# Moving the first batch's transform on chip, with a first MLP block of plain products

## The chip, the cores and the metric

One core of one Trainium2 chip runs the kernel alone. The metric is the device time of one launch in microseconds (us), as the median of several executions. The experiments ran on several chips of the same kind; each was timed beside executions of the kernel before on its own chip, and ratios are against those.

## The reference

Eight batches of 3008 tokens by 256 channels are filtered in the frequency domain, and the result goes through an MLP with a hard-swish. All is float32.

```python
def _attn_ref(x, filt_r, filt_i):                 # x (8, 3008, 256)
    X = np.fft.rfft(x, axis=1)
    Y = X * (filt_r + 1j * filt_i)[None, :, :]
    return np.fft.irfft(Y, n=x.shape[1], axis=1).astype(np.float32)

def _moe_ref(x, w_in, w_out):                     # x (24064, 256), w_in (256, 2048), w_out (2048, 256)
    h = x @ w_in
    g = h * np.clip(h + 3.0, 0.0, 6.0) / 6.0
    return (g @ w_out).astype(np.float32)
```

## The kernel before

The Fourier transform over 3008 = 47 x 64 tokens is done in stages on TensorE. `a_unit` transforms over 47; its output goes to DRAM (`z_tmp`) and comes back in another layout. `b_unit` transforms over 64, `f_unit` multiplies by the filter on VectorE, `y_unit` adds the products up, and `bi_unit` is the first inverse stage. Its output goes through DRAM again (`g_tmp`, loaded by `t4_load`), and `n_unit` is the last inverse stage, which feeds the MLP.

The MLP works on 47 blocks of 512 tokens, in eight steps each (one per 256 hidden columns). A block uses Strassen's scheme: seven 2x2-block products in place of eight, for which VectorE and GpSimd form sums of inputs and weights. The weights come as 64-bit floats and are converted by VectorE with integer operations (`w_conv`).

The first batch is transformed before the MLP starts, in a prelude, and the other batches' stages are spread over the MLP's steps by a plan, `at(step, function, ...)`. The other batches' stages are spread over the MLP's steps by a plan: `at(step, function, ...)`.

```python
        for c in range(NB):                          # prelude, cut
            a_unit(0, c)
            z_store(0, c, (nc.sync, nc.scalar))
            ...
        convert(6)
        for c in range(TB):
            t2_load(0, c)
            ...
        for i in range(NU + 1):
            if i < NU:
                b_unit(0, i)
                f_unit(0, i)                         # three products on VectorE
                y_unit(0, i)                         # two sums on VectorE
                if i % 3 == 2 and i < NU - 1:
                    convert(1)
            ...                                      # bi_unit, g_store, table_load
        ...                                          # t4_load, n_unit; then the MLP
            if n == 1:                               # places of batch 2's stages, in MLP steps
                a_at = list(range(NB))
                b_at = [10 + 7 * i // 4 for i in range(NU)]
            ...
            for c in range(NT):
                s = ... if c >= TB else a_at[-1] + 1
                at(s, t2_load, n, c)                 # nc.sync.dma_start(t, z_d[...])
                s = ... if c >= FB else a_at[-1] + 1
                at(s, table_load, n, c)              # five loads on nc.sync
        ...
            if dn and pd == 0 and kd:                # in the step after a block's last
                out_5(kd - 1)                        # ends with store(): 14 DMAs a block on nc.sync
```

Of the kernel before, what the change touches and what calls it, by code (L numbers as in the profile page):

```python
# [22 lines left out]
N = 3008  # L23
NA = 47
# [30 lines left out]
def _make_tables():  # L55
# [3 lines left out]
    wai = np.zeros((P, HC, TOK))  # L59
    for h in range(2):  # L60
        for k in range(KH):
            th = 2 * np.pi * ((a * k) % NA) / NA
            for g in range(2):
                wa[h * 64:h * 64 + NA, g * 64 + k] = np.cos(th)
                wa[h * 64:h * 64 + NA, g * 64 + 32 + k] = -np.sin(th)
    wb = np.zeros((P, KH, P))
    wi = np.zeros((P, NC))
# [11 lines left out]
    for q in range(64):  # L79
# [3 lines left out]
        wi[q], wi[HALF + q] = ab, sign * ab  # L83
# [14 lines left out]
    return wa.astype(f), (wai / N).astype(f), wb.astype(f), wi.astype(f)  # L98
# [3 lines left out]
def kernel(  # L102
# [11 lines left out]
    wa_np, wai_np, wb_np, wi_np = _make_tables()  # L114
# [3 lines left out]
    wi_d = nc.inline_tensor(wi_np, name="wi_t").ap()  # L118

# [26 lines left out]
    wi = const.tile([P, NC], FP32, name="wi")  # L146
    xs = [const.tile([P, XC, D], FP32, name="xs%d" % i) for i in range(3)]
# [3 lines left out]
    w_in = [const.tile([P, 7, P], FP32, name="w_in%d" % p) for p in range(NP)]  # L151
    w_out = [const.tile([P, 7, P], FP32, name="w_out%d" % p) for p in range(NP)]
# [35 lines left out]

    def w_before(i):
        return i - 4 if i < 10 else i - 2  # L190

    def w_load(i):
        if i < 8 and i % 4 > 1:
            t = gp.tile([P, 7, 256], FP32, name="g").bitcast(I32)[:, 0:4, :].rearrange("p a n -> p (a n)")
        else:
            t = op.tile([P, 1024], I32, name="bits", tag="o")
        nc.gpsimd.dma_start(t.rearrange("p (a d) -> p a d", a=2), w_part(i)[0])
        st["bits", i] = t

    def w_conv(i):  # L200
        words = st.pop(("bits", i)).rearrange("p (n two) -> p n two", two=2)
        lo, hi = words[:, :, 0], words[:, :, 1]
        big, rest = (sp.tile([P, 2, D], FP32, name=s).bitcast(I32).rearrange("p a n -> p (a n)")
                     for s in ("s1", "s2"))
        v = nc.vector
        v.tensor_scalar(out=big, in0=hi, scalar1=3, scalar2=0x3FFFFFFF,
# [6 lines left out]
                        op0=ALU.logical_shift_right, op1=ALU.bitwise_or)  # L213
        rest, big = rest.bitcast(FP32), big.bitcast(FP32)
# [3 lines left out]
        v.tensor_scalar(out=hi, in0=hi, scalar1=20, scalar2=0x7FF,  # L218
                        op0=ALU.logical_shift_right, op1=ALU.bitwise_and)
        high = hi.bitcast(FP32)  # L220
        nc.gpsimd.tensor_scalar(out=high, in0=hi, scalar1=897.0, scalar2=None, op0=ALU.is_ge)
        two = lambda t: t.rearrange("p (a d) -> p a d", a=2)
        nc.gpsimd.tensor_tensor(out=w_part(i)[1], in0=two(rest), in1=two(high), op=ALU.mult)

        w = (w_in, w_out)[i % 2][i // 2]
        for o, x0, x1, op_ in IN_SUMS if i % 2 == 0 else OUT_SUMS:
            nc.gpsimd.tensor_tensor(out=w[:, o, :], in0=w[:, x0, :], in1=w[:, x1, :], op=op_)
# [17 lines left out]

    def x_tile(b, c):
        i = (b * NB + c) % 3
        if b == 0 and 3 <= c < 6:
            return xn.rearrange("p a n -> p (a n)")[:, ts(i, XC * D)].rearrange("p (j d) -> p j d", j=XC)
        return xs[i]  # L250

    def x_load(b, c, q=None):
        q = q or nc.sync
        t = x_tile(b, c)
        rows = x[b].rearrange("(a c) d -> a c d", c=NC)
        for h in range(2):
            for r, n in ((0, 32), (32, NA - 32)):
                q.dma_start(t[h * 64 + r:h * 64 + r + n, :, :], rows[r:r + n, ds(h * HC + c * XC, XC), :])


    def bank(b):
        if b:
            return psF.tile([P, 2, D], FP32, name="psf", tag="f")
        st["bank"] = i = (st.get("bank", -1) + 1) % 4
        return psO.tile([P, 2, 2, P], FP32, name="po%d" % i).rearrange("p a u m -> p a (u m)")
# [478 lines left out]
```

## Time and profile before

| | kernel before |
|---|---|
| time, median of 3 | 2802.28 us (2801.35 to 2804.47) |
| span of the profiled execution | 2800.2 us |
| filter starts / last filter sum ends | 61.23 / 119.17 us |
| MLP starts / its second block starts | 138.24 / 212.74 us |
| 25th MLP step starts | 331.71 us |

The profile is of one execution; times in it run from the span's start. The line numbers (L392) are those of each kernel's own file. TensorE is nearly full from some 140 us to the end, so what the change can win lies in the first part. The lines for this stand in the prediction.

### The profile page before, as it was taken

To read this page: it belongs to the slowest core of one execution; us is meant where nothing else is said; L and a number is where in the kernel's file an instruction comes from. 1 tells how busy PE (TensorE), PEld (TensorE's weight loads), DVE (VectorE), ACT (ScalarE), POOL (GpSimd) and SP (SyncE) were. 2 spreads that over 40 slices of the span, in tenths; PEclk is the share of its full clock that TensorE was granted. 3 is DMA by queue.
4 is the path that set the end of the run, shared out by engine and by line. 5 is a ranking of instruction groups with operands and counts; after the bars stand their busy time and mean duration, and the time that the engine had idled before them with its cause. 6 is when DMAs were issued, how large, how long until landed. Compare 5 with 4: busy or idle time off the path is not lost.

```text
span 2800.2 us, 47225 instructions
## 1 busy us (share of the span) xinstructions
PE 2699.6 (96%) x18096; PEld 2397.0 (86%) x18096; DVE 1994.4 (71%) x3464; ACT 1324.2 (47%) x2672; POOL 459.9 (16%) x670
## 2 busy tenths in 40 slices
PE   4589999999999999999999999999999999999997
PEld 1269888989889998899988998899988999999997
DVE  6787875777757776577766777667775677766665
ACT  1144445454554445544455444554455444444443
POOL 6470112100120111201021101211012100000000
PEclk9699999999999999999999999999999999999999
DMA  7644223321223212222133221332123312110000
GB/s 218 174 111 118 63 55 90 91 68 43 72 74 85 79 50 71 75 77 75 51 82 91 68 61 42 88 88 76 49 54 90 100 52 54 36 32 23 19 8 16
DMA packets 122077, 200.83 MB, mean 72 GB/s; under 512 B 22605, under 2 KB 86829, under 8 KB 121725
## 3 DMA queue, kind: packets, MB, share of 16 engines
q1 hardware_dynamic: 96847, 139.15, 17.5%
q0 software_dynamic: 20032, 52.62, 8.0%
q10 hardware_dynamic: 4974, 6.05, 0.8%
q8 instruction: 143, 2.34, 0.4%
q14 instruction: 81, 0.66, 0.1%
HBM read 122.75 MB, written 74.97 MB: 71 GB/s over the span
## 4 chain that ended last, share of the span: by engine, by line
PE 92%; DVE 3%; DMA 2%; POOL 1%; ACT 1%; issue 1%; SPq 0%; ACTq 0%; POOLq 0%; DVEq 0%
PE po L468 42%; PE al L392 23%; PE be L392 17%; PE psn L367 4%; PE psf L300 3%; PE psf L275 2%; PE psf L329 2%; DMA z_tmp<-t 1%; DMA xn<-in_x_dram 1%; DVE y L319 0%; DMA g_tmp<-t 0%; DVE s L314 0%; DVE s L313 0%; DVE g L442 0%; ACT t L278 0%
## 5 line engine op out<-in xcount | busy, mean ns | idle before, releaser
L468 PEld LDWEIGHTS po<-w_out,g 128*128 128x128 f32 x10528 | 1398.7, 192 | 152.4 <-issue 37.3
L468 PE MATMUL po<-w_out,g 128*128 128x128 f32 x10528 | 1431.0, 276 | 4.9 <-DVE g L442 4.6
L442 DVE SCALAR_TENSOR_TENSOR g<-r,h 128x512 f32<-128x512 f32 x752 | 519.0, 690 | 268.4 <-ACT r L437 255.7
L437 ACT ACTIVATE r<-h,half_c 128x512 f32<-128x512 f32 x752 | 542.6, 722 | 337.6 <-DVE h L418 325.2
L392 PE MATMUL al<-xt,w_in 128*128 128x256 f32 x2256 | 675.5, 381 | 6.2 <-ACT s L413 3.3
L418 DVE TENSOR_TENSOR h<-be,s 128x512 f32<-128x512 f32 x376 | 259.7, 691 | 272.4 <-PE be L392 250.7
L392 PE MATMUL be<-xn,w_in 128*128 128x256 f32 x1504 | 447.8, 379 | 0.0
L392 PEld LDWEIGHTS al<-xt,w_in 128*128 128x128 f32 x2256 | 342.7, 192 | 9.3 <-ACT s L413 3.4
L392 PEld LDWEIGHTS be<-xn,w_in 128*128 128x128 f32 x1504 | 286.1, 190 | 38.9
L432 ACT ACTIVATE h<-al 128x256 f32<-128x256 f32 x376 | 144.1, 383 | 355.5 <-PE al L392 355.5
L423 DVE TENSOR_TENSOR h<-al,s 128x256 f32<-128x256 f32 x376 | 159.6, 424 | 167.5 <-PE al L392 166.1
L450 DVE TENSOR_TENSOR g<-g 128x512 f32<-128x512 f32 x376 | 260.2, 692 | 12.9
L413 ACT ACTIVATE s<-al 128x256 f32<-128x256 f32 x376 | 144.3, 384 | 199.7 <-PE al L392 199.7
L404 ACT ACTIVATE s<-be 128x256 f32<-128x256 f32 x376 | 144.1, 383 | 181.4 <-PE be L392 181.4
L392 PE MATMUL al<-xn,w_in 128*128 128x256 f32 x752 | 225.2, 381 | 0.5 <-ACT h L432 0.5
L392 PE MATMUL be<-xt,w_in 128*128 128x256 f32 x752 | 224.1, 380 | 0.0
L288 POOL DMA_DIRECT2D z_tmp<-t x224 | 131.5, 591 | 417.2 <-ACT t L278 407.7
L452 DVE TENSOR_TENSOR g<-g 128x256 f32<-128x256 f32 x376 | 168.8, 449 | 12.8
L403 ACT ACTIVATE s<-al 128x256 f32<-128x256 f32 x376 | 144.1, 383 | 70.5 <-PE al L392 70.5
L449 DVE TENSOR_TENSOR g<-g 128x256 f32<-128x256 f32 x376 | 161.9, 431 | 12.8
L495 POOL TENSOR_TENSOR o<-p,o 128x256 f32<-128x256 f32 x46 | 33.4, 726 | 833.9 <-ACT t L332 361.2
L392 PEld LDWEIGHTS be<-xt,w_in 128*128 128x128 f32 x752 | 143.2, 190 | 19.4
(76 smaller groups left out, 1788.0 us busy)
## 6 DMA issues: line engine op xcount, KB each, us to landing
t<-z_tmp SPq DMA_DIRECT2D x48, 512.0 KB
t<-g_tmp SPq DMA_DIRECT2D x188, 120.0 KB
z_tmp<-t POOLq DMA_DIRECT2D x224, 96.0 KB, 3.2
g_tmp<-t POOLq DMA_DIRECT2D x84, 256.0 KB, 3.8
xs<-in_x_dram SPq DMA_DIRECT2D x120, 128.0 KB
out_dram<-o SPq DMA_DIRECT2D x321, 47.0 KB
ft<-in_filt_r_dram SPq DMA_DIRECT2D x96, 128.0 KB
ft<-in_filt_i_dram SPq DMA_DIRECT2D x96, 128.0 KB
```

The source lines that it names most:

```text
L392: nc.tensor.matmul(ps, w_in[p][:, w, :], x, start=start, stop=stop, skip_group_check=True)
L403: nc.scalar.activation(out=s[:, 0, :], in_=al, func=AXT.Copy)
L404: nc.scalar.activation(out=s5, in_=be[:, 1, :], func=AXT.Copy)
L413: nc.scalar.activation(out=s[:, 1, :], in_=al, func=AXT.Copy)
L418: nc.vector.tensor_tensor(out=st["h"][0].rearrange("p (a n) -> p a n", a=2), in0=be, in1=s, op=ALU.add)
L423: nc.vector.tensor_tensor(out=st["h"][1][:, 256:512], in0=al, in1=s5, op=ALU.add)
L437: nc.scalar.activation(out=r, in_=st["h"][i], func=AXT.Relu, bias=half_c, scale=1.0 / 6.0)
L442: nc.vector.scalar_tensor_tensor(out=st["g", k, p][:, o:o + 2, :].rearrange("p a n -> p (a n)"), in0=st["r", i], scalar=1.0, in1=st["h"][i ...
L449: v.tensor_tensor(out=g[:, G1, :], in0=g[:, G3, :], in1=g[:, G22, :], op=ALU.add)
L450: v.tensor_tensor(out=g[:, G3:G2 + 1:2, :], in0=g[:, G3:G1 + 1, :], in1=g[:, G11:G11 + 1, :].broadcast_to([P, 2, 256]), op=ALU.subtract)
L452: v.tensor_tensor(out=g[:, G4, :], in0=g[:, G12, :], in1=g[:, G2, :], op=ALU.subtract)
L468: nc.tensor.matmul(st["po", k][bank][:, part, u, :], g[:, a, ts(u, P)], w_out[p][:, w, :], start=(p == 0 and n in OPENS and u == 0), stop= ...
```

## The change

The intent has three parts. (1) The first batch's first two stages stay on chip: x is laid out so that one product of a 96-column table gives the transform over 47 with the channel on the partitions, and further products against the identity ("turns") bring it to `b_unit`'s layout, without `z_tmp`. (2) For batch 1, the sums of `y_unit` move into the weights of the inverse (`wi` gets three forms). (3) The MLP's first block runs as eight plain products: no sums of inputs or weights are needed for it, VectorE has time for conversions, and the sums of weights on GpSimd come later. With these go new places for conversions (five fewer before the MLP), a delay for batch 2's stages, and, in `plain_out`, the first block's output in the ninth step.

```diff
+    def a0_unit(j):
+        for dh in range(2):
+            ps = bank(0)
+            for u in range(4):
+                t, o = x0_tile(j + u)
+                nc.tensor.matmul(ps[:, ds(u * 96, 96)], t[0:2 * NA, o, ts(dh, P)], st["start"][0:2 * NA, ds(P, 96)], ...)
+            nc.scalar.activation(out=zt(dh).rearrange("p (n j) -> p j n", j=HC)[:, j:j + 4, :],
+                                 in_=ps[:, 0:384].rearrange("p (j n) -> p j n", j=4), func=AXT.Copy)
+    def turn(c):
+        ...   # per chunk: 8 products zt(dh)[:, ts(k, P)] by the identity, 2 evictions
@@ bi_unit
-                nc.tensor.matmul(ps[ri][ts(v, 64)], wi[ts(ri, 64), :], ys[v][ts(ri, 64)], start=True, stop=True)
+                w, y = (wi[ts(ri, 64), 0, :], ys[v][ts(ri, 64)]) if b else (wi[:, 1 + ri, :], ys[v][ri])
+                nc.tensor.matmul(ps[ri][ts(v, 64)], w, y, start=True, stop=True)
@@ first block
+    def plain_up(p):    # 4 products of 512 columns, 2 activations
+    def plain_down(p):  # 8 products of 256 columns
+    def plain_out():
+        ...                      # two evictions
+        store(0, 0, 4)
@@ the plan
-            at(i, convert, 1)
+            at(i // 2, convert, 1)
+        for p in range(NP):
+            at(p + 2, w_sums, p)
-                a_at = list(range(NB))
-                b_at = [10 + 7 * i // 4 for i in range(NU)]
+                a_at = list(range(1, NB + 1))
+                b_at = [11 + 18 * i // 11 for i in range(NU)]
@@ a step of the second block
+            if last_plain:
+                plain_down(pd)
+                plain_out()
```

(Cut: loads of x into the later weight tiles on both hardware queues, the new order of table and weight loads, a conversion that gives one operation to ScalarE.)

## The prediction

> **What bounds the kernel now.** I read the page's slices first, to see where TensorE is not full.
>
> ```profile
> PE   4589999999999999999999999999999999999997
> PEclk9699999999999999999999999999999999999999
> ```
>
> One slice is 70 us. From the third slice to the last, TensorE is 90% busy or more, and the change leaves that work alone. All it can win lies in the first three slices, where the first batch is transformed before the MLP has anything to eat. So I next read TensorE's timeline of the first 215 us (start, length, line, records; a float32 product is two records).
>
> ```profile
> 42.66 2.47 PE L275 MATMUL po<-xs,wa 64*64 64x512 f32 x8 [4.35 <-ACT t L278]
> 59.15 3.68 PE L300 MATMUL po<-t,wb 128*128 128x256 f32 x8 [14.02 <-DMA t<-z_tmp]
> ...
> 118.50 1.79 PE L329 MATMUL psf<-y,wi 64*64 64x512 f32 x4 [1.07 <-DVE y L319]
> 132.50 4.98 PE L367 MATMUL psn<-wai,t 128*128 128x94 f32 x22 [12.21 <-DMA t<-g_tmp]
> 137.70 0.74 PE L367 MATMUL psn<-wai,t 128*128 128x94 f32 x2 [0.23 <-ACT xn L373]
> 138.24 1.12 PE L392 MATMUL al<-xn,w_in 128*128 128x256 f32 x2
> ...
> 212.74 0.60 PE L392 MATMUL al<-xn,w_in 128*128 128x256 f32 x2
> ```
>
> This gives four stages: the first transform and the trip through DRAM (0 to 59.15 us), the second stage with filter and inverse (59.15 to about 118.5), a tail of store, load and last transform (to 138.24, where the MLP starts), and the MLP's first block of eight steps (138.24 to 212.74, 74.5 us; the first product of each step marks it). To see what fills them I read busy time by stage (length, then PE, weight load, DVE, ACT, POOL, clock, DMA share, GB/s):
>
> ```profile
> 20.00:40.00 20.00, 11.44 (x40) 2.64 (x38) 19.23 (x26) 4.44 (x9) 18.93 (x21) 1.00 0.83 223
> 40.00:60.00 20.00, 3.32 (x10) 1.38 (x11) 3.31 (x5) 3.26 (x6) 14.51 (x18) 1.00 0.77 233
> ...
> 80.00:100.00 20.00, 15.51 (x35) 6.11 (x34) 18.79 (x29) 2.39 (x4) 6.71 (x9) 0.67 0.63 180
> 100.00:120.00 20.00, 13.78 (x32) 4.72 (x29) 18.79 (x29) 2.79 (x5) 5.99 (x7) 0.74 0.40 110
> ...
> 160.00:180.00 20.00, 17.49 (x112) 13.68 (x112) 18.51 (x29) 9.04 (x18) 16.96 (x23) 1.00 0.45 130
> ```
>
> Before 59 us DMA is the bound (about 0.8 of its engines; in the chain of waits the long pieces there are loads of x and stores to z_tmp). From 60 to 120 us, and again in the first MLP block, it is VectorE, 18.5 to 18.8 of 20 us.
>
> **What the Trainium skill says.** (1) "TensorE: Matmul & The Clock Gate", Part 1: an idle array gets half the clock, and one busy window of about 3.4 us lifts that. The trace agrees: the 64x512 group at 42.66 took 2.47 us, the same group at 140.99 took 1.13. But from 134.3 to 137.7, a full window of 94-column products, the granted clock stayed 0.50; it rose at 141.1, after 256-column products. Short products behind a weight load may not count as busy enough. (2) Same page, "LDWEIGHTS": time goes by the weights' columns. In the trace a 94-column product costs as much as a 128-column one: ten records in 1.09 us full, 22 in 4.98 us at half clock, 0.109 and 0.226 us a record. So a short product costs 0.22 us, 0.45 us cold. (3) "TensorEngine Tiling (Array Packing)", Key Properties: tiles of the array work independently. Four 64x64x512 products took 1.02 us together, against 0.85 us for one. The new inverse has 64 columns but all 128 rows; no run here shows whether two such overlap.
>
> **The change, part by part.**
>
> *x arrives.* Now 3.08 MB of x go on both hardware queues in 8 KB rows, with 1.05 MB of weights on the third. At 4 to 16 us the profile shows 262 to 278 GB/s; I take 268 from 2.6 us on. ScalarE issues half of these loads. In the issue timeline its loads of x lasted from 6.06 to 17.69 us, each waiting for a load eight places earlier to land, and only then did it load its table (1.28 us) and evict. The new order gives the same: its last issue waits for the fourteenth load, so for 2.5 + 1.05 MB, 2.6 + 3.55/0.268 = 15.8 us; with issue and table, the first eviction is at about 18 us.
>
> *First stage, 64 products of 96 columns.* Four banks allow two of the eight units before that eviction (they fit between 7 and 15 us even cold). The other six are 48 products: 48 x 0.45 = 21.7 us cold, 10.4 us warm. By (1) I choose cold: this stage ends at about 40 us (warm from its middle, 32). Evictions (128x384, 0.49 us) hide behind it.
>
> *Turning.* 48 products of 128 columns against the identity, eight per chunk of four k: 1.74 us warm, 3.6 cold. The first two chunks come before any filter work: 7 us, so the first filter multiply is near 47.5 us. The trip through z_tmp (store, load, 49 to 59 us above) is gone. So the filter starts 14 us earlier (61.2 before).
>
> *Filter stage.* y's sums go (12 x 2 x 0.69 + gaps = 17 us of VectorE), as do one conversion there and five in all before the MLP. Left are 36 operations of 0.69 us with gaps, 12 x 2.15 = 25.8 us, and two conversions of eight operations: 0.43 + 0.75 + 0.43 + 0.35 + 0.35 + 0.69 + 0.69 + 0.70 and gaps = 4.5 us each. Sum 35 us. TensorE per chunk of two units: turn 1.74, four 256-column products 1.71, inverse 4 x 0.85 = 3.4 if nothing overlaps: 6.8 us, six times 41 us, of which the first turns lie before and the last inverse after. So both engines need about 35 us here; with their waits on each other and some half clock I take 37: filter ends at 85 us.
>
> *Tail.* From the end of the last filter work to the MLP it was 138.24 - 118.45 = 19.8 us (inverse 1.8, eviction 0.6, store 4.1, issues 3.5, load 3.8, transform 5.7). Same pieces now, inverse perhaps 1 us longer: 20.5. The MLP starts at 105 to 106 us, **33 us earlier** than 138.24.
>
> *First MLP block.* Plain costs more TensorE: 4 x 0.85 + 8 x 0.43 = 6.8 us a step against 14 x 0.43 = 6.0. But VectorE is the bound: ten conversions are left instead of five, two per step in steps 0 to 4, of 4.2 us each (one operation now ScalarE's), plus two activations of 0.69 with gaps (1.45) where there were seven operations (about 4.6): 9.85 us a step. The sixth step's first activation frees the bank at about 7.4 + 5 x 9.7 = 56 us after the MLP starts; then two steps at TensorE's 6.8 + 1.0 (first transform of batch 2) = 7.8: step eight at 71.5 us, plus some 2 us for stores to z_tmp that now queue on GpSimd behind weight loads and sums: 73.5, against 74.5 before. The ninth step holds the last plain product, +0.4 us.
>
> *After that* the two programs run the same instructions; batch 2's later stages move by one step, hidden behind MLP work. Sum: 2802.3 - 33 - 1 + 0.4 = 2768.7, rounded to **2768 us**.
>
> **Rivals.**
> (a) *The first stage warms up.* For: it runs unbroken for 20 us. Against: the window at 134.3. It makes the filter start some 9 us earlier: 2759. With overlapping inverses, 2755.
> (b) *TensorE becomes the bound of the filter stage at half clock.* Before, the clock there flickered (0.67 and 0.74 above) because TensorE waited for VectorE; a conversion still leaves it idle for about 4 us. Then a chunk costs up to 13 us, if for two or three of them: MLP at 115, 2779.
> (c) *GpSimd chokes the first block.* Each step gives it eight weight sums of 0.555 us and four stores' issues of 0.59, 6.8 us, and loads ahead of them that wait for conversions. ScalarE waits for a t1 buffer, holds the activations, and TensorE stands. ScalarE lost 10.0 us to that wait before. 5 to 12 us more: 2775 to 2780.
> (d) *DMA bounds the filter stage.* Tables, weights, g_tmp and the inverse's table are about 9 MB between 20 and 85 us, 140 GB/s against 270 possible; a table's 768 KB has about 8 us. I give it little; 2773 if so.
>
> **Range and chances.** (a) alone gives 2755 to 2759, (b) and (c) together 2787. A range of 2752 to 2786 holds what I think of. For faster by over 2% the time must fall under 2746, so the MLP start under some 84 us; with 20 us of tail and 35 of VectorE work behind a load that ends at 18 to 20 us, that needs a first stage hidden wholly under the load. 6%. Slower by over 2% would need the saved trip to DRAM to be lost twice over: 1%.
>
> **What would show it.** In the changed profile's timeline: ScalarE's first eviction near 18 us; the 96-column records 0.226 us apart (0.109 would be rival a); first filter multiply near 47 us; last one near 85; first product of the MLP near 105 (the main number); nine to ten us per step in steps 1 to 5 of the first block with VectorE at 18 or more of 20 us, then about 8; the third slice on as before. The prediction is wrong if the MLP starts before 90 or after 115, or if the first block takes over 80 us, or if TensorE shows new waits after it.

## The result, and the profile after

The changed kernel took **2790.13 us** (2789.14 to 2791.65, 4 runs), the kernel before in the same rounds 2803.24 us (2801.35 to 2804.47, 4 runs). The ratio is 0.9954, with a 95% interval of 0.9937 to 0.9972. (A ratio here is the mean time of one kernel's runs over that of the other's of the same rounds, so not quite the ratio of the medians quoted.) So it is faster by 0.5%; predicted were 1.2%, and the time lies 4 us above the range.

The page of the changed kernel, TensorE's busy total and its two rows of 40 slices:

```profile
PE 2714.4 (97%) x18112; PEld 2420.2 (87%) x18112; DVE 1940.1 (70%) x3399; ACT 1330.6 (48%) x2663; POOL 398.4 (14%) x627
...
PE   7698999999999999999999999999999999999997
PEclk9899999999999999999999999999999999999999
```

The first three slices are fuller (7, 6, 9 in place of 4, 5, 8), and the clock of the second (PEclk, the TensorE clock that was granted, in tenths of full speed) is an 8 in place of a 6. But the fourth slice, from 209 to 279 us, was a 9 and is an 8: there is a hole in it. TensorE's timeline of the changed kernel (start, length, line, records; in brackets the idle time ahead of it and what ended it):

```profile
8.00 7.11 PE L295 MATMUL po<-p,w_all 94*128 94x96 f32 x32 [8.00 <-DMA w_all<-in_x_dram]
23.78 17.39 PE L295 MATMUL po<-p,w_all 94*128 94x96 f32 x80 [8.67 <-ACT xn L297]
...
56.85 1.94 PE L382 MATMUL psf<-s,wi 128*64 128x512 f32 x8
...
81.56 3.65 PE L350 MATMUL po<-t,wb 128*128 128x256 f32 x8 [2.21 <-DMA wb<-wb_t]
...
104.42 4.98 PE L420 MATMUL psn<-wai,t 128*128 128x94 f32 x22 [14.19 <-DMA t<-g_tmp]
109.62 0.74 PE L420 MATMUL psn<-wai,t 128*128 128x94 f32 x2 [0.23 <-ACT xn L426]
110.15 3.02 PE L532 MATMUL al<-xn,w_all 128*128 128x512 f32 x4
...
168.24 3.78 PE L532 MATMUL al<-xn,w_all 128*128 128x512 f32 x4 [3.93 <-DVE g L495]
...
187.30 0.59 PE L445 MATMUL al<-xn,w_all 128*128 128x256 f32 x2
...
218.61 2.05 PE L350 MATMUL psf<-t,wb 128*128 128x256 f32 x4 [7.20 <-DMA ft<-in_filt_r_dram]
```

The MLP starts at 110.15 us and its second block at 187.30. The last line is the new thing: in the twelfth step TensorE stands for 7.2 us for a filter table of batch 2. Set side by side, with the start of the same MLP step in both traces as the marks:

| stage | before, us | after, us | gain | gain predicted |
|---|---|---|---|---|
| start to first filter multiply | 61.2 | 52.6 | 8.6 | 13.7 |
| filter stage | 57.9 | 35.25 | 22.7 | 20 |
| tail to the MLP's start | 19.1 | 22.3 | -3.2 | -0.7 |
| first block, 8 steps | 74.5 | 77.15 | -2.65 | 1 |
| steps 9 to 24 | 118.97 | 134.94 | **-15.97** | -0.4 |
| the rest | 2468.5 | 2467.7 | 0.8 | 0 |
| sum | 2800.2 | 2789.9 | 10.3 | 33.6 |

(The filter stage ends with VectorE's last operation of it: before, the second of the last two sums, at 119.17 us; after, the last product, at 87.85.)

Of the 28.1 us that the MLP starts earlier, 16 are given back in sixteen steps that were to be "hidden". The sync queue's own timeline shows why. Before the change (the issues of batch 2's loads, then the first block's output):

```profile
213.80 0.40 SPq L293 DMA_DIRECT2D t<-z_tmp  x1
...
220.01 0.34 SPq L169 DMA_DIRECT2D wb<-wb_t  x1
220.68 0.39 SPq L293 DMA_DIRECT2D t<-z_tmp  x1
223.81 13.19 SPq L516 DMA_DIRECT2D out_dram<-o  x14
```

and after it:

```profile
194.44 13.66 SPq L598 DMA_DIRECT2D out_dram<-o  x14
208.42 0.40 SPq L343 DMA_DIRECT2D t<-z_tmp  x1
...
216.82 0.39 SPq L176 DMA_DIRECT2D wb<-wb_t  x1
217.47 0.39 SPq L343 DMA_DIRECT2D t<-z_tmp  x1
```

The two have changed places. The first block's tokens lie in 14 runs of up to 47 rows of the output, so its store is 14 DMAs, and issuing them took the queue 13.2 to 15.8 us in the runs shown here, whatever stood behind. Before, the loads were planned for the ninth step and the store fell in the tenth. The change moved the store to the ninth and the loads to the tenth. They are issued at 208 to 217 us, while the second stage of batch 2 wants them in the twelfth step, from 210 us.

The start of the kernel, by busy time of the changed kernel (columns as in the prediction's table):

```profile
0.00:20.00 20.00, 7.11 (x32) 6.90 (x32) 4.58 (x11) 0.00 (x0) 4.46 (x9) 1.00 0.93 193
20.00:40.00 20.00, 16.22 (x76) 16.22 (x77) 4.03 (x8) 11.18 (x14) 1.06 (x2) 1.00 0.78 210
...
60.00:80.00 20.00, 16.08 (x87) 10.06 (x86) 19.28 (x32) 6.00 (x12) 0.00 (x0) 1.00 0.86 241
```

The DMA engines are busy 0.93 of the first 20 us and move only 193 GB/s (223 at 0.82 before); from 2.6 us on, the stretch that the prediction's sum is about, it was 210 GB/s. (The clock column reads 1.00 in the first two rows though the products there run at half clock; the trace has no record of the clock before 50.93 us. How long a record takes is the better sign.) ScalarE's timeline of the changed kernel:

```profile
0.74 14.22 ACTq L285 DMA_DIRECT2D w_all<-in_x_dram  x8
18.21 2.19 ACTq L285 DMA_DIRECT2D t<-in_x_dram  x2
21.20 0.36 ACTq L624 DMA_DIRECT2D wi<-wi_t  x1
21.59 1.28 ACT L297 ACT_TABLE_LOAD   x1 [21.59 <-DMA t<-in_x_dram]
22.89 0.84 ACT L297 ACTIVATE xn<-po 128x384 f32<-128x384 f32 x1
```

ScalarE is tied up until 21.56 us, by its share of x's loads and by the load of `wi`, and loads its function table only then. Little of that is issuing: the ten issues of loads of x took 0.32 to 0.68 us each, 3.8 us together. The rest is waiting until earlier loads have landed (four issues went out by 2.7 us, the next at 4.66, 6.82, 12.78 and 14.63). Its first eviction is at 22.89 us where 18 was predicted, and TensorE waits 8.67 us for it.

### The profile page after: what moved, and what is told of

Same layout as the page of the kernel before. It is cut to its first block, busy times and chain, and to the rows that moved or that the text cites. A ratio compares the mean times of both kernels' runs of the same rounds, so it can differ in the third digit from the quotient of the medians.

```text
span 2789.9 us, 47067 instructions
## 1 busy us (share of the span) xinstructions
PE 2714.4 (97%) x18112; PEld 2420.2 (87%) x18112; DVE 1940.1 (70%) x3399; ACT 1330.6 (48%) x2663; POOL 398.4 (14%) x627
## 4 chain that ended last, share of the span: by engine, by line
PE 93%; DVE 3%; DMA 2%; SPq 1%; POOL 1%; issue 0%; ACT 0%; POOLq 0%; ACTq 0%; DVEq 0%
PE po L521 41%; PE al L445 22%; PE be L445 17%; PE psn L420 4%; PE psf L350 3%; PE psf L327 2%; PE psf L382 2%; PE po L295 1%; DMA w_all<-in_x_dram 0%; SPq L413 0%; DVE g L495 0%; PE po L350 0%; DMA out_dram<-o 0%; DMA wb<-wb_t 0%; DVE y L224 0%
## 5 line engine op out<-in xcount | busy, mean ns | idle before, releaser
L521 PEld LDWEIGHTS po<-w_all,g 128*128 128x128 f32 x10304 | 1368.7, 191 | 143.4 <-issue 36.5
L521 PE MATMUL po<-w_all,g 128*128 128x128 f32 x10304 | 1399.1, 276 | 3.7 <-DVE g L495 3.3
L445 PE MATMUL al<-xt,w_all 128*128 128x256 f32 x2208 | 660.2, 381 | 1.5 <-DVE h L476 1.0
L445 PE MATMUL be<-xn,w_all 128*128 128x256 f32 x1472 | 437.8, 379 | 0.0
L445 PEld LDWEIGHTS al<-xt,w_all 128*128 128x128 f32 x2208 | 335.5, 192 | 3.5 <-issue 1.3
L445 PEld LDWEIGHTS be<-xn,w_all 128*128 128x128 f32 x1472 | 279.7, 190 | 37.9
L503 DVE TENSOR_TENSOR g<-g 128x512 f32<-128x512 f32 x368 | 254.8, 692 | 12.6
L445 PE MATMUL al<-xn,w_all 128*128 128x256 f32 x736 | 219.9, 381 | 0.5 <-ACT h L485 0.5
L445 PE MATMUL be<-xt,w_all 128*128 128x256 f32 x736 | 218.9, 379 | 0.0
L502 DVE TENSOR_TENSOR g<-g 128x256 f32<-128x256 f32 x368 | 156.5, 425 | 12.6
L445 PEld LDWEIGHTS be<-xt,w_all 128*128 128x128 f32 x736 | 139.8, 190 | 18.9
L420 PEld LDWEIGHTS psn<-wai,t 128*128 128x128 f32 x1024 | 134.1, 195 | 22.2 <-issue 16.0
```

What stands on the lines that cost most here:

```text
L420: nc.tensor.matmul(ps[:, ts(q, TOK)], t4[i % 2][:, q, ts(dh, P)], wai[:, chunks[i][1] + q, :], start=True, stop=True)
L445: nc.tensor.matmul(ps, w_in[p][:, w, :], x, start=start, stop=stop, skip_group_check=True)
L502: v.tensor_tensor(out=g[:, G1, :], in0=g[:, G3, :], in1=g[:, G22, :], op=ALU.add)
L503: v.tensor_tensor(out=g[:, G3:G2 + 1:2, :], in0=g[:, G3:G1 + 1, :], in1=g[:, G11:G11 + 1, :].broadcast_to([P, 2, 256]), op=ALU.subtract)
L521: nc.tensor.matmul(st["po", k][bank][:, part, u, :], g[:, a, ts(u, P)], w_out[p][:, w, :], start=(p == 0 and n in OPENS and u == 0), stop= ...
```

## The experiments

Fifteen kernels ran, all with correct results. Two theories were open at first for the 16 us: the order of the sync queue (A), or the second stage's new places in the plan and a DMA system that is simply full (B). For the start: x's loads on ScalarE's queue, and the clock.

### The store behind the loads (e1_store_later)

```diff
 def plain_out():
-        store(0, 0, 4)
 ...
+            if n == 1:
+                at(a_at[-1] + 1, store, 0, 0, 4)     # after batch 2's first loads
```

> The changed kernel with one line moved: the output store of the MLP's first block is issued behind batch 2's first loads (z_tmp, filter, table) on the sync queue instead of ahead of them. Theory A (the gain was given back on the sync queue: 14 small stores took it from 194.44 to 208.10 us, and the loads behind them came 7.2 us too late for TensorE in the twelfth step): the 7.2 us wait goes, and with it the half clock after it; steps 9 to 24 of the MLP shrink from 134.9 us by 8 to 12, and the time falls to 2778 to 2782. Rival B (batch 2's stores to z_tmp, which queue on GpSimd behind the weight sums, are what is late: the last was issued at 196.3): the load of z_tmp still waits for them, the wait moves and shrinks by 2 us at most, time 2788 to 2790.

Measured: **2780.15 us** (2779.39 to 2781.23), ratio 0.9919 [0.9904, 0.9934]; the changed kernel stands at 0.9954, so some 10 us less. The sync queue's timeline of this run:

```profile
196.48 0.40 SPq L343 DMA_DIRECT2D t<-z_tmp  x1
...
203.33 0.39 SPq L343 DMA_DIRECT2D t<-z_tmp  x1
203.93 15.81 SPq L597 DMA_DIRECT2D out_dram<-o  x14
```

TensorE's timeline has the same products of the twelfth step, with no bracket, so with no wait:

```profile
209.61 1.06 PE L350 MATMUL psf<-t,wb 128*128 128x256 f32 x4
```

The twelfth step took 8.13 us, as before the change, against 16.99; steps 9 to 24 took 126.1 us against 134.94. Theory A holds for this step, and B falls: the places in the plan are the same here, and the wait is gone. The rival in the expectation, late stores of `z_tmp` on GpSimd, falls too: by it the wait would have stayed. What follows for the 15.97 us: 8.86 were the twelfth step: 7.2 us of wait, and half clock, which began in the wait and held the first 3 us of products after it (218.6 to 221.6 us). Another 3.02 are the ninth step (9.17 us against 6.15): it holds the first block's last plain products and a first-stage unit of batch 2 that stood in the eighth before. The remaining 4.1 us, which this run still loses, are in the main small waits of 0.3 to 0.7 us: TensorE stands 4.2 us in steps 10 to 24 of this run, against 1.4 us before. What sets those was not tested; the closer places of the second stage's units are one candidate.

### x's loads off ScalarE's queue (e3_x_sync)

```diff
-            for h, q in ((0, nc.sync), (1, nc.scalar)):
+            for h, q in ((0, nc.sync), (1, nc.sync)):
 ...
-        nc.scalar.dma_start(wi, wi_d)
+        nc.sync.dma_start(wi, wi_d)
```

> The changed kernel with all loads of the first batch's x (and the inverse's weights) issued by the sync queue, none by ScalarE. Theory A (the first stage stood still from 15.1 to 23.8 us because ScalarE was issuing loads until 21.6 and then loaded its table, so no bank was emptied): ScalarE evicts as soon as the first unit is done, near 9 us, TensorE runs through at half clock from 8 to about 37 us, filter starts 6 to 8 us earlier than 52.6, time 2782 to 2785. Rival B (the data themselves were late, DMA moved 193 GB/s in the first 20 us): TensorE waits for loads instead, filter starts at most 3 us earlier, and with one queue x may arrive even later.

Measured: **2784.7 us** (2784.03 to 2785.99), ratio 0.9935 [0.9918, 0.9951]. ScalarE's timeline of this run, then TensorE's:

```profile
0.74 1.28 ACT L297 ACT_TABLE_LOAD   x1 [0.74 <-PEq L819]
12.46 0.83 ACT L297 ACTIVATE xn<-po 128x384 f32<-128x384 f32 x1 [10.44 <-PE po L295]
```

```profile
10.43 24.18 PE L295 MATMUL po<-p,w_all 94*128 94x96 f32 x112 [10.43 <-DMA w_all<-in_x_dram]
```

The table is loaded at once, the first eviction follows the first products, and the 8.67 us of wait are gone. The MLP starts at 103.88 us, 6.3 earlier. One queue fed TensorE without a gap. With two queues the first products had started earlier (8.00 us against 10.43), and that was all that the second one brought. The Trainium skill, "DMA: Bandwidth & Descriptors", section "Issuing engines are not separate DMA queues", says that starting DMAs on several engines saves only the time to start them, "which is usually small relative to the DMA itself". For these loads the trace agrees: of the 14.22 us that eight of them held ScalarE, the issues were 3.2, and the rest was the wait for earlier loads. For the store of the first block it does not: 14 small DMAs held the sync queue for 13.66 us, of which the issues themselves were 12.7, single ones 0.25 to 2.57 us.

### Warming the clock (e4_warm, e11_warm2, e13_warm20)

The 80 records of 96 columns took 17.39 us, 0.2135 us from the start of one to the next: half clock, over an unbroken run of 20.6 us. Only after 128-column turns did the clock rise, at 50.93 us. So rival (a) did not come about. The question was whether such products can run at full clock at all. The first try put twelve 256-column products between the second and third unit, each into its own tile of one bank:

```diff
         for j in range(0, HC, 4):
             a0_unit(j)
+            if j == 4:
+                for u in range(12):
+                    nc.tensor.matmul(psU.tile([P, 512], FP32, name="al")[:, 0:256], st["start"][:, 0:P],
+                                     st["start"][:, 0:256], start=True, stop=True)
```

> The changed kernel with twelve 256-column dummy products on TensorE between the second and third unit of the first stage, where it idles from 15.1 to 23.8 us; results unused. In the changed kernel the six later units ran 20.6 us without a gap at half clock (0.2135 us a record). Theory A (the array had not been lifted to full clock because 94-row, 96-column products behind weight loads do not count as busy enough to lift it, but do count enough to hold it): records 0.109 to 0.12 us apart, the first filter multiply 8 to 10 us earlier than 52.6, time 2780 to 2783. Rival B (such products do not hold the full clock either): the clock falls back after one or two windows of 3.4 us, the filter starts at most 4 us earlier. Rival C (evictions of 0.84 us each, two a unit, become the bound at 1.7 us a unit): unit period 1.7 to 1.9 us, which is hardly to be told from A by time but by TensorE's waits.

Measured: 2796.76 us, ratio 0.9978 [0.9963, 0.9993]. It failed as a test. TensorE's timeline of this run:

```profile
14.70 15.19 PE L647 MATMUL al<-p 128*128 128x256 f32 x24
29.68 17.22 PE L295 MATMUL po<-p,w_all 94*128 94x96 f32 x80
```

Each product took 1.27 us where 0.85 is half clock's time: there is one buffer for that tile, so each product has to wait until the one ahead has left it (argued from the code; the next run, without that wait, agrees). TensorE was not dense, the clock did not rise, and all came 6 us later. The second try lets the twelve accumulate in one tile:

```diff
+                warm = psF.tile([P, 512], FP32, name="psf", tag="f")
+                for u in range(12):
+                    nc.tensor.matmul(warm[:, ts(u % 2, 256)], st["start"][:, 0:P], st["start"][:, 0:256],
+                                     start=u < 2, stop=u > 9, skip_group_check=True)
```

> The dummies again, now accumulating into one bank that is never handed on (in e4_warm each took 1.27 us, as it waited for the one before to drain, so TensorE was never dense and the clock never rose). Twelve 256-column products from 15 us on: about eight at half clock (6.8 us), four at full. Theory A (96-column products hold a full clock, they only cannot lift it): first-stage records about 0.11 to 0.12 us apart after the dummies, filter starts near 43 instead of 52.6, time 2780 to 2783. Rival B (they do not hold it): clock falls again within two windows, 2786 to 2790. If the dummies do not lift the clock at all: as the changed kernel, 2789 to 2792.

Measured: 2784.5 us median, ratio 0.9942 [0.9918, 0.9965], but in two groups: 2776.35 and 2779.36, 2789.64 and 2790.96. The profiled execution is the first. TensorE's timeline:

```profile
14.45 7.46 PE L648 MATMUL psf<-p 128*128 128x256 f32 x24
22.25 9.17 PE L295 MATMUL po<-p,w_all 94*128 94x96 f32 x80 [0.34 <-ACT xn L297]
```

The clock rose at 18.67 us, and the same 80 records took 9.17 us in place of 17.39. So in these runs 96-column products held the full clock while they followed each other without a gap, but did not raise it. The MLP started at 94.60 us. The mean granted clock was 0.991 and 0.990 in the two fast executions, and 0.987 and 0.986 in the two slow ones, so more time at half clock; where in the execution isn't known, as neither was profiled. The third try, with twenty products, tests whether twelve were too few for some positions of the clock's window:

> The experiment with twelve 256-column products between the second and third unit, with twenty in place of twelve. Twelve gave two groups of times, 2776 to 2779 and 2790 to 2791, the slow ones with a lower mean granted clock (0.987 against 0.991). Theory: twelve products last about 7.5 us cold, which holds one whole window for some positions of the clock's window and none for others; twenty last long enough for any position, so all four runs lie in one group at 2776 to 2782, with a mean granted clock of about 0.99. Rival: the two groups come from something else (the arrival of x, or a later wait): twenty products give two groups again, or all at 2785 and above.

Measured: **2780.3 us** (2778.09 to 2781.84), ratio 0.9913 [0.9898, 0.9928], one group, mean clock 0.991 in all four. TensorE's timeline:

```profile
14.52 11.03 PE L648 MATMUL psf<-p 128*128 128x256 f32 x40
25.38 9.07 PE L295 MATMUL po<-p,w_all 94*128 94x96 f32 x80
```

The numbers came as the theory forecast: with twelve products two of four executions were slow, with twenty none of four. The Trainium skill, "TensorE: Matmul & The Clock Gate", Part 1, says that the window of some 3.4 us is free-running and that the same kernel measures differently with its position. The traces agree in part: the clock's changes lie whole multiples of 3.41 us apart (in the changed kernel at 50.93, 81.65, 85.07 and 95.31 us).

But that this made the two groups is not shown. The theory took 7.5 us as the time of twelve cold products, and that was measured with the clock rising midway. At 0.85 us each they last 10.2 us cold (an estimate), so a full window of 3.41 us fits in wherever it starts. A rival was not tested: after the twelve, TensorE waits for ScalarE's first eviction (0.34 us above), and in the slow executions, which were not profiled, a longer wait may have let the clock fall again. After the twenty there is no wait. b3, told below, shows that such products can lose the clock: behind waits of 0.34, 0.31 and 1.30 us it fell at 27.59 us, for 6.8 us. And four executions each, on two different chips, are few.

### The filter sums back on VectorE (e7_y_back)

```diff
-  w, y = (wi[ts(ri, 64), 0, :], ys[v][ts(ri, 64)]) if b else (wi[:, 1 + ri, :], ys[v][ri])
+  w, y = wi[ts(ri, 64), 0, :], ys[v][ts(ri, 64)]
 ...
                     f_unit(0, i)
+                    y_unit(0, i)
```

(And buffers moved so that it fits.)

> The changed kernel with the filter sums of batch 1 back on VectorE (two 64x512 operations a unit, 24 in all) and the inverse as four 64x64 products a pair. If the inverse's weights took 17 us off VectorE on the path: filter stage 35.25 us becomes 50 to 53, time 2804 to 2807 (the whole gain and more). Rival: TensorE or the tables' loads bound that stage as well (TensorE was busy 29.05 of 35.25 us and waited for tables three times), then it grows by 10 us or less, time under 2800.

Measured: 2805.28 us (2804.3 to 2806.35), ratio 1.0008 [0.9993, 1.0023]: all of the gain is gone. The filter stage took 51.8 us (51.26 to 103.10) against 35.25, and the MLP started at 123.25. So the sums in the inverse's weights are worth 15 us of the whole time in this kernel, close to the 17 us of the prediction's sum.

### The inverse alone, in the kernel before (e10_inverse_only)

Here the kernel before gets only the three forms of `wi`, with `y_unit` dropped for batch 1.

> The kernel before with one part of the change alone: batch 1's filter sums in the inverse's weights. If VectorE alone bounds the filter stage (54.19 of 57.25 us busy), it loses 24 operations, 17 us: stage 40 to 43 us, time 2785 to 2789. Rival (loads of tables, z_tmp and weights bound it next): stage 46 to 52 us, time 2792 to 2798. The blocks after it are the ones of before, so nothing should be given back later.

Measured: **2794.73 us** (2790.18 to 2795.7), ratio 0.9967 [0.9952, 0.9982]. The filter stage took 47.6 us (57.9 before), not the 40 to 43 of the theory. TensorE's timeline shows the rival's reason:

```profile
86.02 2.08 PE L301 MATMUL po<-t,wb 128*128 128x256 f32 x4 [8.80 <-DMA wb<-wb_t]
...
101.96 1.89 PE L301 MATMUL po<-t,wb 128*128 128x256 f32 x4 [4.71 <-DMA wb<-wb_t]
```

With VectorE faster, tables that were in time before come too late. The MLP starts 7.0 us earlier, and 6.15 of that are still there at the second block, the 25th step and after: the order of the sync queue is the old one here, and little is given back. (The places in the plan are the old ones too, so this run does not tell theory A from B; e1 does.)

### The first block as seven products (e9_seven)

```diff
-            if k == 0:
+            if k < 0:                      # never: no plain block
 ...
-        convert(2, False)
+        convert(4, False)
+        for p in range(4):
+            w_sums(p)
 ...
-            at(p + 2, w_sums, p)           # for p in range(NP)
+            at(p - 4, w_sums, p)           # for p in range(4, NP)
```

> The changed kernel with the MLP's first block as seven products a step again (sums of weights behind their conversions on GpSimd; four conversions in the tail before the block, eight in its steps 0 to 3). To be held against e5_conv4, which has the same conversions and the plain block. If the plain block is worth having because it takes some 3 us a step off VectorE while that is the bound: block of 80 to 85 us here against 66 to 70 in e5_conv4, time 10 us or more over it. Rival (TensorE's 0.9 us a step more and the late sums eat it): both within 4 us.

Measured: 2809.99 us (2807.83 to 2811.92), ratio 1.0025 [1.001, 1.004]. The first block took 92.24 us; busy time of the engines in it:

```profile
108.69:200.93 92.24, 71.22 (x386) 54.56 (x385) 65.84 (x108) 35.99 (x73) 52.60 (x89) 0.83 0.40 109
```

Its first five steps took 13.8 to 14.6 us, each with a conversion whose weights the sums, and then the products, wait for. So with conversions left for the first block, the plain one is worth some 19 us: this run has four conversions in the tail, like the next one, whose block took 73.23 us. (The kernel before came to its first block, also of seven products, with five conversions left, not eight.) After the block this run loses another 14 us in its twelfth step, where TensorE waits 12.4 us for a filter table: the store falls in the tenth step here, with the loads, but ahead of them. This is one more sign for theory A.

### Conversions, GpSimd's sums, and the first block (e5_conv4, e12_sums_late)

The first block took 77.15 us, not 73.5. Steps 2 to 5 lasted 9.9 to 10.8 us, near the predicted 9.85; the sixth and seventh took 12.3 and 10.96, with the wait of 3.93 us at 168.24 in the timeline above, for VectorE's part of the activation. The first try does two more conversions in the tail (`convert(2, False)` becomes `convert(4, False)`):

> The changed kernel with four instead of two weight conversions in the tail before the MLP, where VectorE idles from 96.5 to 113.9 us, so eight instead of ten in the first block. If VectorE is the block's bound in steps 1 to 5 (9.9 us a step, two conversions each), the block falls by one such step's excess and more: 77.15 us becomes 66 to 71, MLP start unmoved near 110; but the store on the sync queue still stands before batch 2's loads, so that only part arrives: time 2781 to 2787. Rival (GpSimd's sums and stores bound it): block over 74 us, time over 2787.

Measured: 2786.25 us (2783.91 to 2789.6), ratio 0.9944 [0.9927, 0.996]. The block took 73.23 us, between the theory's and the rival's numbers. Fewer conversions did not help by the 4.2 us each that they should: the fourth and fifth steps still took 11.0 and 12.6 us.

VectorE's groups in the changed kernel, first from 125 to 145 us, then from 145 to 168 us (busy us, mean ns of one):

```profile
L237 DVE SCALAR_TENSOR_TENSOR y<-y 128x512 f32<-128x512 f32 x4 | 2.8, 692 | 0.1
L222 DVE TENSOR_SCALAR y<-bits 128x512 int32<-128x512 int32 x2 | 0.8, 420 | 0.0
```

```profile
L237 DVE SCALAR_TENSOR_TENSOR y<-y 128x512 f32<-128x512 f32 x4 | 3.6, 894 | 0.1
L222 DVE TENSOR_SCALAR y<-bits 128x512 int32<-128x512 int32 x2 | 1.4, 689 | 0.0
```

The same operations are slower in the second stretch, in which GpSimd is busy 22.05 of 23 us with sums of weights and inputs and with stores (6.64 of 20 us in the first). The Trainium skill, "GPSIMD Engine Reference", section "1. Specifications", says that its SBUF interfaces are shared with VectorE, with contention against operations of two SBUF inputs or in a two-port mode. To test that this is the cause, the sums move four steps on, behind the conversions:

```diff
-            at(p + 2, w_sums, p)
+            at(p + 6, w_sums, p)
```

> The changed kernel with the weight sums of a slice placed four steps later (from the seventh step on instead of the third), so that GpSimd runs no sums beside the conversions. Main theory: the conversions are slowed by GpSimd's sums beside them (0.89 us against 0.69 for a two-operand operation in steps 3 to 5). Then those operations stay at about 0.69 us, TensorE's wait of 3.9 us in the seventh step goes, and the first block takes 72 to 74 us instead of 77.15; time about 3 to 5 us under the changed kernel's, 2785 to 2787. Rival: the slow conversions have another cause (the DMA traffic, the stores to z_tmp), or the sums stand in the way later: block 76 us or more, or the gain is lost in steps 9 to 16.

Measured: **2784.87 us** (2782.51 to 2785.59), ratio 0.9928 [0.9913, 0.9943]. The block took 72.28 us, the sixth and seventh steps 9.6 and 8.2. VectorE's groups of this run from 145 to 165 us:

```profile
L237 DVE SCALAR_TENSOR_TENSOR y<-y 128x512 f32<-128x512 f32 x4 | 2.8, 692 | 0.1
```

So the weight sums beside the conversions cost the first block 4.9 us. Their absence doesn't make every operation fast: GpSimd still forms four sums of inputs (L438) here, from 149.29 to 153.44 us, and issues stores to `z_tmp` after them. VectorE's conversion beside the two, with GpSimd's first of each kind, from this run's timeline:

```profile
148.95 1.37 DVE L222 TENSOR_SCALAR y<-xt 128x512 int32<-128x512 int32 x1
149.29 0.74 POOL L438 TENSOR_TENSOR xt<-xn 128x256 f32<-128x256 f32 x1
...
153.38 2.31 POOL L339 DMA_DIRECT2D z_tmp<-t  x4
...
154.02 0.69 DVE L237 SCALAR_TENSOR_TENSOR y<-y 128x512 f32<-128x512 f32 x1
```

L222 took 1.37 us beside a sum, in place of 0.42; beside the issues of stores L237 took its 0.69. So it is GpSimd's sums that slow VectorE, and not the stores that the expectation's rival named. The slowing is only about half of the 4.9 us: the ten conversions' operations took 45.7 us in the changed kernel's block and 43.3 here, and the last of them ended 57.4 and 55.3 us after the block's start. The other 2.7 us came behind it, where in the changed kernel the clock fell to half from 167.0 to 173.8 us, after TensorE's wait of 3.93 us; here it stayed full. ScalarE's wait for a `t1` buffer, 3.8 us in the changed kernel, is gone as well; what it took part in was not separated. Nothing is lost later: steps 9 to 24 took 133.2 us (134.94).

### Three without a gain (e8_x_4k, e6_t4_act, b2_all)

x came in 8 KB rows; the first run has it in 4 KB rows (`for j in range(0, HC, 4): x0_load(j, 4)`).

> The changed kernel with the first batch's x loaded in rows of 4 KB (eight groups of four positions) instead of 8 KB. In the first 20 us the changed kernel moved 193 GB/s with its DMA engines 93% busy, the kernel before 223 at 82%, with 4 KB rows. If the long rows are what costs (a packet of 8 KB took about 610 ns, one of 4 KB about 240 in the kernel before), x is complete 2 to 4 us earlier, ScalarE's first eviction is at 19 to 21 instead of 22.9, time 2786 to 2788. Rival (the traffic as a whole is the limit, whatever its rows; and with at most eight loads in flight, half the size each, it may get worse): no change, 2789 to 2792, or slower.

Measured: 2791.32 us, ratio 0.9955 [0.994, 0.997]: nothing. x comes a little faster (213 GB/s at 0.82 in the first 20 us against 193 at 0.93), but ScalarE now has 16 issues, and the first eviction is at 22.32 us.

In the tail, the sync queue issues 16 loads of `g_tmp`. In the second run ScalarE issues eight of them.

> The changed kernel with the last eight of the sixteen loads of g_tmp in the tail issued by ScalarE instead of the sync queue, which took 11.54 us to issue them (0.6 to 0.77 us each). Theory (issuing is the tail's bound: both stores had landed by about 95 us, the issues went on to 104): tail from last filter operation to MLP 22.3 becomes 18 to 19.5, MLP start near 106, time 2785 to 2788. Rival (issues of the two queues wait for each other, as at most eight loads are under way): tail over 21, time over 2788.

Measured: 2791.71 us, ratio 0.9954 [0.9937, 0.9971]: nothing. The issues in the changed kernel (sync queue):

```profile
92.41 11.54 SPq L413 DMA_DIRECT2D t<-g_tmp  x16
```

In this run the sync queue issued eight from 88.23 us on, for 7.52 us, and ScalarE eight from 91.06, for 8.48. The issues end at 99.5 us instead of 103.95, but the sync queue starts batch 2's loads of x at 97.07 us now, and they share the engines with the rest of `g_tmp`; the tail took 23.6 us (22.3). (That the sharing is what ate the gain is argued.)

The third is told with the next one.

### The best version (b1_store_sync_warm, b2_all, b3_sums_late)

b1 takes the store behind the loads, x on one queue, and sixteen 256-column products at the very start, while x is still on its way:

```diff
+        warm = psF.tile([P, 512], FP32, name="psf", tag="f")
+        for u in range(16):
+            nc.tensor.matmul(warm[:, ts(u % 2, 256)], st["start"][:, 0:P], st["start"][:, 0:256],
+                             start=u < 2, stop=u > 13, skip_group_check=True)
         for j in range(0, HC, 4):
             a0_unit(j)
```

> The changed kernel with three mends together: output of the first block behind batch 2's loads, x issued by the sync queue alone, and sixteen dummy 256-column products from about 3.5 us on, so that TensorE is dense until x comes and the clock is lifted before 14 us, whatever the phase of its window. If the three losses are separate: first stage follows the loads and ends near 25 to 28 us, filter starts at 30 to 33 (52.6), 20 us gained there, 10 at the store: time 2758 to 2764. Rival (the first two tables now arrive too late, near 31 us, or the clock falls while TensorE waits for x): filter starts at 36 to 42, time 2766 to 2772.

Measured: **2763.81 us** (2761.47 to 2767.55), the kernel before beside it 2802.73; ratio **0.9859** [0.9844, 0.9874]. TensorE's timeline:

```profile
2.88 9.70 PE L644 MATMUL psf<-p 128*128 128x256 f32 x32 [2.88 <-DMA p<-start_t]
12.42 12.64 PE L295 MATMUL po<-p,w_all 94*128 94x96 f32 x112
```

The clock is full from 8.04 us, the filter starts at 32.4 (its first multiply waits for a filter table's load by then, so the rival holds in part, without the cost that it forecast), the MLP at 88.36, and of the 49.9 us of lead there, 39.8 are left from the 25th step on. The executions' times follow their mean clock: 2761.47 at 0.994 to 2767.55 at 0.991.

b2 adds two conversions in the tail, half of the `g_tmp` issues on ScalarE, and the weight sums behind the stores to `z_tmp` on GpSimd:

> As b1_store_sync_warm, and four conversions in the tail instead of two, the tail's last loads on ScalarE, GpSimd's weight sums behind its stores in each step. If each keeps what it gave alone (conversions 4 us, tail 3, sums 2): time 6 to 10 us under b1, 2750 to 2758, under 2% faster than before or just at it. Rival (one bound takes the place of another in the first block, VectorE's conversions still being there): less than 4 us under b1.

Measured: 2768.45 us (2760.89 to 2773.19), ratio 0.9872 [0.9852, 0.9891]; no better than b1. b3 is b1 with the later weight sums of e12:

> The best kernel so far (store later, x on one queue, sixteen early products) with the weight sums four steps later. If the sums slow the conversions: 3 to 5 us under that kernel, 2758 to 2761 by its median of 2763.8. If they do not, or stand in the way later: 2763 or more.

Measured: 2763.3 us (2758.15 to 2765.31), beside 2803.31; ratio 0.9849 [0.9832, 0.9866]. The block did become shorter (73.5 us against 77.5 in b1's profile), but b1's and b3's intervals overlap. In b3's profiled execution x came at 195 GB/s in the first 20 us (212 in b1's), TensorE had to wait for it, and the MLP started 5.6 us later. The two ran on different chips; which is better is open. Both beat both kernels.

## Why the prediction was wrong, point by point

The gain was predicted at 33.6 us and measured at 10.3 in the traces: 23.3 us less. Three slips of the prediction stand in its text. Its 118.45 us is the end of the last filter sum but one; the last ended at 119.17, so the tail before was 19.1 us and not 19.8. Rival (c)'s 5 to 12 us more than 2768 are 2773 to 2780, not 2775 to 2780. And "later stages move by one step" holds for the first stage and the first loads only (see the change).

**The step that failed** is "After that the two programs run the same instructions; batch 2's later stages move by one step, hidden behind MLP work." The instructions are the same, but their order on the sync queue is not. The store, moved one step ahead, and the loads, moved one step back, changed places, and TensorE stood in the twelfth step: 8.9 us, shown by e1. I had looked at what moved on each engine, not at what moved on the queue, which no engine's busy share shows. e1, with nothing but this put right, took 2780.15 us, inside the range. The same sentence hid another 4.1 us, in the main small waits (cause open). "The ninth step holds the last plain product, +0.4 us" was 3.0: the first-stage unit of batch 2 that moved there, and 1.1 us of waits, were left out.

**x arrives**: predicted first eviction 18 us, measured 22.9. The mechanism was right (ScalarE issues and waits for loads, loads its table, then evicts), the term was not: 268 GB/s were assumed from 2.6 us on, 210 came. In the prediction's own sum this makes 2.6 + 3.55/0.210 = 19.5 us in place of 15.8 (an estimate), 3.7 of the 4.9 us. e3 shows that ScalarE's share of the loads need not be in the way at all. With it the start to the first filter multiply is 5.1 us long of the 47.5.

**First stage cold**: right, 0.2135 us a record against 0.226 (which was a group's whole length over its records), and rival (a) did not occur; but e11 and b1 show that it was to be had.

**Turning and the inverse**: the four 128-row, 64-column products of 512 columns took 1.94 us, not 3.4. So two of them do overlap, which the prediction had left open.

**Filter stage**: right, 35.25 us against 37, VectorE busy 33.35 of it. Rival (d) shows as waits of 1.4 to 2.2 us for `wb` in the timeline, rival (b) as one stretch of 3.4 us at half clock; neither made the stage longer than predicted. That the stage hangs on VectorE's operations is shown by e7.

**Tail**: 22.3 us against 20.5. The last two stores to `g_tmp` are only 2.7 us apart now (88.27 and 90.93), and all 16 load issues come after them, from 4.6 us after the filter's end on, for 11.54 us; before, the two stores were 6.7 us apart (114.23 and 120.95), and the issues began at 119.05, ahead of the last store and 0.1 us before the filter's end. e6 shows that splitting the issues alone does not win this back.

**First block**: 77.15 us against 73.5. The step's 9.85 us was right while GpSimd was quiet. Rival (c) named the right engine and 5 us as its lower size, but only part of the way: ScalarE's waits for a buffer were 3.8 us, the longest 3.1. Of the 4.9 us that e12 took away, some 2.4 are GpSimd's sums slowing VectorE's conversions, which the prediction did not have, and the rest came behind them, with the half clock and the waits; these were not separated.

The terms together, measured less predicted: 5.1 - 1.75 + 1.8 up to the MLP, 3.65 in the block, 2.6 in the ninth step, 8.9 in the twelfth, 4.1 in others, less 0.8 in the rest, make 23.6, against 23.3 to be explained.

What stays open: the 4.1 us in steps 10 to 24, whether b1 or b3 is the better, and what made e11's two groups. What part (1), the stages on chip, is worth alone was not run by itself; the 8.6 us are read from the stages.

## What to carry to other kernels

When a change moves work by a step, compare the order on each DMA queue before and after, not only on the engines: a store in many small pieces that slips ahead of loads delays them by its whole issue time. An engine that issues loads can't evict until its issues are through, and most of that time can be waiting for earlier loads; ask what the second queue brings for it. Ahead of a long run of narrow products, give TensorE a dense run of wide ones, with no gap between the two, at a time when TensorE would wait anyway, and look in the trace whether the clock rose and stayed.

## What the Trainium skill lacked or had wrong

- "TensorE: Matmul & The Clock Gate", Part 1: it speaks of a busy window, but not of what is dense enough to count. An unbroken run of 20.6 us of 96-column products did not raise the clock; the same products held it once raised, as long as they followed without a gap (80 records in 9.17 us against 17.39; in b3 it fell again behind waits of up to 1.30 us). 256-column products that each waited for the one ahead (1.27 us instead of 0.85) did not raise it in 15.19 us.
- The same page, "LDWEIGHTS (loading the stationary operand)": one time is given, without the clock. In a stream of 96-column products a record took 0.115 us at full clock (9.17 us for 80) and 0.2135 at half clock.
- "TensorEngine Tiling (Array Packing)", Key Properties: right, but with no number for the 128-row, 64-column form. Four such products of 512 columns took 1.94 us, where four times one product's 0.85 would be 3.4.
- "DMA: Bandwidth & Descriptors", "Issuing engines are not separate DMA queues": the time to start a DMA is called usually small. For loads of 8 KB rows that fits (0.32 to 0.68 us each). But 14 stores of at most 47 rows held the sync queue for 13.66 us, 12.7 of it the issues, single ones up to 2.57 us. And the page's section doesn't say that an engine whose next load waits for earlier ones stands still for so long: eight loads held ScalarE for 14.22 us, 3.2 of it issuing.
- "ScalarE: Activation LUTs", "What ACT_TABLE_LOAD costs": an operation's time is given by the number of elements alone. A 128x384 eviction that writes with a stride took 0.81 to 0.89 us, where the page's 186 ns + 0.833 ns an element would make 0.51 (an estimate); in the kernel before, one of 128x384 that writes without a stride took 0.49. No run isolates the stride.
- "GPSIMD Engine Reference", section 1: the contention is named without a size. Beside GpSimd's sums a two-input operation of VectorE went from 0.692 to 0.894 us in the mean of four, a one-input one from 0.420 to 0.689 in the mean of two, and in e12 a one-input one took 1.37 beside a sum. Beside GpSimd's issues of stores they were not slower (0.69).
